# Two cached attentions on one core: Q regrouped by fewer matmuls, one reciprocal for two quads, another table of rankings

## The chip, the cores and the metric

The kernel runs on one core of one Trainium2 chip. The metric is the device time in microseconds (us) of one execution. A time of the kernel is the median of its runs. Engines in the profile: PE is the matmul engine and PEld its weight loads, DVE the vector engine, ACT the scalar engine, POOL the general-purpose engine, SP the engine that issues nearly all loads.

## The reference

Two attention blocks over cached keys and values, each with a query projection and an output projection, side by side in the output. Block A shares each of 4 key/value heads among 8 query heads; block B has 32 key/value heads for its 32 query heads. All inputs and the output are bfloat16.

```python
def _B_ref(x, k_cache, v_cache, wq, wo):        # x: 16 x 32 x 1024
    B, Sq, D = x.shape
    H, Dh = 32, 128                             # k_cache, v_cache: 16 x 32 x 1024 x 128
    q = (x @ wq).reshape(B, Sq, H, Dh).transpose(0, 2, 1, 3)
    scores = jnp.einsum("bhqd,bhkd->bhqk", q, k_cache) * (Dh ** -0.5)
    p = _softmax(scores, axis=-1)
    o = jnp.einsum("bhqk,bhkd->bhqd", p, v_cache)
    return o.transpose(0, 2, 1, 3).reshape(B, Sq, H * Dh) @ wo

# _A_ref: the same with 4 key/value heads, each repeated for 8 query heads
return jnp.concatenate([a, b], axis=-1)         # 16 x 32 x 2048
```

## The kernel before

**Work.** The 512 tokens form 4 groups of 128 (G). Block A has 128 "quads", each the work of one batch entry and 4 query heads (128 rows of scores against 1024 keys). Block B has 128 quads too, taken in pairs: a pair covers two batch entries and four heads. The keys and values of B are read once and used once: 256 K tiles and 256 V tiles of 512 KB each, which are most of the bytes. K tiles of B have 8 slots (`KB_sb`), V tiles 6 (`VB_sb`). In late steps further K and V tiles go into the space of `wq_sb`, `xT_sb`, `QT_sb`, and the last four V tiles into `KB_sb`.

**A quad.** Scores on PE (A: line 995, B: line 1027 on 32x32 tiles of the array, 64 matmuls a pair in four calls), a negated row maximum on DVE (L1038), the exponential on ACT with the row sum as its side output (L1051), transposes of P on PE (A: L1063, B: L1097) with their copies out of PSUM on ACT or DVE (L651), P times V on PE (A: L1083, B: L1116 on 64x64 tiles; the last pair in two halves, L1135), the reciprocal of the sum on DVE (L1165), the scaling by it on ACT or DVE (L1174, L1175), a transposition of the output on PE (A: L1182, B: L1190), and its copy out. B's K tiles are transposed in place by DVE in blocks of 32x32 (L976). After each group the output projection (L823) adds to `acc` (L835, L844); the last adds (L839) are followed by the last stores (L841).

**Sums.** The row maximum, the sum and the reciprocal of every quad lie in one slot of `stat` (8 slots of 4 columns). In B the two quads of a pair share one tile of P (`P2_sb`, one slot, or space in `xT_sb`).

**Q of block B.** For each of the 32 groups of a block of 4 heads, the projected queries (`Qtok`, L754) are transposed by DVE in 32x32 blocks into `QBt` (`qprepB_tr`, L765) and then put into the four row groups that the scores need (`qprepB_sh`, L778): matmuls with a 32x32 corner of the identity as the stationary operand, on 32x32 tiles. They are issued as two operations, `Qshuf` (row groups 0 and 2) and `Qshuf2` (1 and 3), each of 8 matmuls; `Qshuf2` waits on a semaphore for `Qshuf`. Two copies out of PSUM make `QR`.

**Order.** The program is written as a list of 4948 operations. A list scheduler (`list_schedule`) then goes through it on the host and places one operation after the other, with prices written in the code (`DUR`, `PE_MODE`, `MODE_IN`, `MODE_OUT`), slots for the PSUM banks and tiles (`SLOTS`), a model of the load queue and of the fetching of PE's instructions. Among the operations that could start at about the same time it takes the one of highest rank. There are 16 ways of ranking (`RANKS`). Every 77 placed operations (`WINDOW`) a table, `TUNE`, says which of the 16 is used next:

```python
turn = len(order) // WINDOW
turn = TUNE[turn] if turn < len(TUNE) else 0
bl, look, act_first = ranks[turn], RANKS[turn][2], RANKS[turn][4]
```

The result is a fixed order for every engine, with semaphores between engines. SP issues the loads in that order, and waits at a load until the readers of its buffer's last content are done. Such a wait holds every later load.

Of the kernel before, what the change touches and what calls it, by code (L numbers as in the profile page):

```python
# [33 lines left out]
PE_INSTR = {"scoresB": 32, "scoresA": 2, "PT_trA": 8, "PT_trB": 8, "PVA": 16, "PVB": 32, "PVBh": 32, "OT_tr": 2, "OT_trB": 4, "KTA_tr": 16, "Qshuf": 16, "Qshuf2": 16,  # L34
            "qprojA": 4, "qprojB": 4, "oprojA": 4, "oprojB": 4, "xT_tr": 16}
FETCH_BLOCK = 252
FETCH_US = 6.2
# [3 lines left out]
PAIR_COST = 0.01  # L41
FREE_BANKS = 2
WINDOW = 77
RANKS = ((3.5, 122, 0.35, 0.0, 0.3), (3.0, 122, 0.35, 0.0, 0.3), (4.0, 122, 0.35, 0.0, 0.3), (3.5, 122, 0.15, 0.0, 0.3), (2.5, 122, 0.35, 0.0, 0.3), (5.0, 122, 0.35, 0.0, 0.3),
         (3.5, 122, 0.7, 0.0, 0.3), (3.5, 120, 0.35, 0.0, 0.3), (3.0, 124, 0.2, 0.0, 0.3), (3.5, 122, 0.15, 1.5, 0.3), (3.5, 122, 0.15, -1.5, 0.3), (3.5, 122, 0.15, 0.0, 0.0),
         (3.5, 122, 0.15, 0.0, 0.7), (3.5, 122, 0.15, 4.0, 0.3), (3.5, 122, 0.15, -4.0, 0.3), (3.5, 122, 0.25, 0.0, 0.3))
TUNE = (6, 7, 1, 5, 6, 8, 8, 8, 8, 8, 8, 11, 5, 15, 1, 9, 0, 1, 5, 1, 7, 14,
        15, 12, 12, 10, 12, 12, 15, 3, 12, 14, 7, 13, 13, 13, 13, 13, 7, 6, 10, 1, 12, 10,
        3, 12, 0, 11, 9, 12, 7, 13, 12, 11, 12, 3, 4, 10, 14, 9, 9, 10, 4, 0, 0)
HOLD_AHEAD = 1  # L50
STEP_NEAR = 0
TAIL_BASE = 12.0
# [6 lines left out]

DUR = {  # L60
    "scoresB": (0.232, 0.20), "scoresA": (0.216, 0.20), "PT_trA": (0.48, 0.22), "PT_trB": (0.48, 0.22), "PVA": (0.45, 0.22), "PVB": (0.437, 0.22), "PVBh": (0.22, 0.22),
    "OT_tr": (0.056, 0.22), "OT_trB": (0.112, 0.22), "KTA_tr": (0.45, 0.22), "Qshuf": (0.39, 0.20), "Qshuf2": (0.235, 0.20), "qprojA": (0.432, 0.20), "qprojB": (0.432, 0.20),
    "oprojA": (0.432, 0.20), "oprojB": (0.432, 0.20), "xT_tr": (0.45, 0.22),
    "exp": (1.10, 0.12), "PT_ev@act": (0.466, 0.13), "norm@act": (0.25, 0.13), "normB@act": (0.36, 0.13), "OT_ev@act": (0.11, 0.13), "OTB_ev@act": (0.17, 0.13), "KTA_ev@act": (0.466, 0.13),
    "qA_ev@act": (0.47, 0.13), "qB_ev@act": (0.478, 0.13), "QR_ev@act": (0.478, 0.13), "acc0@act": (0.47, 0.13), "acc0@dve": (0.58, 0.12), "xT_ev@act": (0.90, 0.13),
# [46 lines left out]
        self.idx = 0  # L112


SLOTS = {"bank": 8, "P": 2, "P2": 1, "PT": 2, "PT2": 2, "stat": 8, "O": 2, "O2": 3}


def actual(res):
# [9 lines left out]
class Prog:  # L128
# [120 lines left out]
    def list_schedule(self, lat=0.05, look=LOOK):  # L249
# [303 lines left out]
def build(nc, pa, pb, out):  # L553
# [34 lines left out]
    with stack:  # L588
# [49 lines left out]
        pr.add("pool", lambda g: g.memset(rowsel[:], 0.0), writes=["rowsel"], name="c0")  # L638
# [129 lines left out]
        def qprepB_sh(m_, G):  # L768
            gp = (m_ * NG + G) % 2
            vv = [Virt("bank", "pj"), Virt("bank", "pj")]  # L770

            def e_sh(e, aa):
                last = None
                for a in aa:
                    out_ = bank(vv[a // 2])[:, (a % 2) * 2 * Dh:(a % 2 + 1) * 2 * Dh].rearrange("p (hp x) -> p hp x", hp=2)
                    src_ = QBt[32 * a:32 * a + 32, :].rearrange("p (hp e x) -> p e hp x", hp=2, e=2)
                    for rg in range(4):
                        last = e.matmul(out_[32 * rg:32 * rg + 32], ident[32 * a:32 * a + 32, 32 * a:32 * a + 32], src_[:, rg // 2, :, :],  # L778
                                        start=True, stop=True, tile_position=(32 * a, 32 * rg))
                return last  # L780
            for name, aa in (("Qshuf", (0, 2)), ("Qshuf2", (1, 3))):
                pr.add("pe", lambda e, aa=aa: e_sh(e, aa), reads=["QBt", "ident"], writes=vv, claims=[("QR", gp, a) for a in aa], name=name,
                       rtag={"QBt": (m_, G)})
# [225 lines left out]
        def st_scoresB(qs):  # L1009
            n = qs[0].pn  # L1010
            vP, vPT = (("xT", 0, 0), (("xT", 0, 1), ("xT", 0, 2))) if n >= XT_FREE and n % 2 else (Virt("P2"), (Virt("PT2"), Virt("PT2")))
            for q in qs:
                score_buf(q)
                q.vP, q.vPT, q.vO = vP, vPT, Virt("O2")
            q0 = qs[0]
            gp = (q0.m * NG + q0.G) % 2

            def e_s(e, fp):
                last = None
                o0 = (fp // 2) * 64 + fp % 2  # L1020
                for x in range(4):
                    for q in qs:
                        for g2 in range(2):
                            r0 = 32 * (2 * q.e + g2)
                            lhsT = QR[r0:r0 + 32, gp, 2 * q.bp + x // 2, x % 2, o0:o0 + 63:2]
                            rhs = tile_k(4 * q.pn + x)[r0:r0 + 32, :].rearrange("p (s x) -> p s x", s=16)[:, :, o0:o0 + 63:2]
                            last = e.matmul(bank(q.vS[g2])[32 * x:32 * x + 32, :].rearrange("p (s j) -> p s j", s=16), lhsT, rhs,  # L1027
                                            start=(fp == 0), stop=(fp == 3), tile_position=(r0, 32 * x))
# [12 lines left out]
        def st_exp(q):  # L1041
            vS, vP, vst = q.vS, q.vP, q.vst

            def emit(e):
                if q.pi == 0:
                    src = both(vS).rearrange("p u (c k) -> p k u c", c=NCH // 2)
                    dst = P_sb[:, vP.idx, :].rearrange("p (k u c) -> p k u c", u=2, c=NCH // 2)
                else:
                    src = both(vS).rearrange("p g (s j) -> p g j s", s=16)
                    dst = p2_of(vP)[:, q.e * Sk:(q.e + 1) * Sk].rearrange("p (g j s) -> p g j s", g=2, s=16)  # L1050
                return e.activation(dst, src, ACTF.Exp, bias=stat[:, vst.idx, 0:1], scale=1.0, accum_out=stat[:, vst.idx, 1:2])  # L1051
            pr.add("act", emit, writes=vS + [vP, vst], name="exp")

        NPK = NCH // 2

# [67 lines left out]
        def st_last(qs):  # L1123
# [16 lines left out]
            for i in range(2):  # L1140
# [4 lines left out]
                for q in qs:  # L1145
# [1 line left out]
                    if i == 0:  # L1147
                        st_recip(q)

                    def emit(e, i=i, vst=vst, vO=vO, vb=vb):  # L1150
                        dst, src = O2_sb[:, vO.idx, i, :], bank(vb)[:, 0:Dh]
                        if hasattr(e, "activation"):
                            return e.activation(dst, src, ACTF.Copy, scale=stat[:, vst.idx, 2:3])
                        return e.tensor_scalar(dst, src, stat[:, vst.idx, 2:3], None, ALU.mult)
                    eng = ("act", "dve")[q.e]
                    pr.add(eng, emit, reads=[vst], writes=[vb, vO], name="norm@" + eng)
# [5 lines left out]

        def st_recip(q):
            vst = q.vst
            pr.add("dve", lambda e: e.reciprocal(stat[:, vst.idx, 2:3], stat[:, vst.idx, 1:2]), writes=[vst], name="recip")  # L1165

        def st_norm(q):
            vst, vO, vb = q.vst, q.vO, q.vbo

            def emit(e):  # L1170
                dst = O_sb[:, vO.idx, :] if q.pi == 0 else O2_sb[:, vO.idx, :, :].rearrange("p i d -> p (i d)")
                src = bank(vb)[:, 0:Dh if q.pi == 0 else 2 * Dh]
                if hasattr(e, "activation"):
                    return e.activation(dst, src, ACTF.Copy, scale=stat[:, vst.idx, 2:3])  # L1174
                return e.tensor_scalar(dst, src, stat[:, vst.idx, 2:3], None, ALU.mult)  # L1175
            pr.add("any", emit, reads=[vst], writes=[vb, vO], name="norm" if q.pi == 0 else "normB")

        def st_otr(q):
            vO, vb = q.vO, q.vbo
# [223 lines left out]
```

## Time and profile before

| | |
|---|---|
| three runs | 850.86, 853.56, 855.13 us; median 853.56 |
| the profiled execution's own time | 848.26 us |
| its span, first to last instruction | 846.5 us |
| granted clock of PE, mean | 0.998 |
| busy | PE 780.7 us (92%), DVE 727.1 (86%), ACT 623.7 (74%), POOL 6.1 (1%) |
| moved by DMA | 341.68 MB, mean 404 GB/s |
| row maxima L1038 | 256, 1210 ns each |
| K transposes L976 (into `KB_sb`) | 240, 1223 ns each |
| exponentials L1051 (into `P_sb`) | 246, 1123 ns each |
| P times V of B, L1116 | 3584 matmuls with `VB_sb`, 271 ns each |

The span is cut into 40 equal slices in the page; a digit is the busy share of a slice in tenths. Durations of matmuls overlap: PE is a pipeline, and a matmul's row shows how long one took from its start to its modelled end, while the next may have begun. The chain of waits follows the work that ended last back to the start, step by step, to what released it. A group's row reads: line, engine, operation, output and inputs, shapes, how many | busy time, mean ns of one | idle time of the engine just before them, and what ended it. A timeline's row reads: start in us, length in us, engine, line, operation, how many were merged, and in brackets the idle time before.

### The profile page before, as it was taken

What the parts mean: (1) busy time and instruction counts of PE and PEld (TensorE: products, weight loads), DVE (VectorE), ACT (ScalarE), POOL (GpSimd) and SP (SyncE); (2) the same over time, 40 slices, a digit from 0 to 9 for tenths busy, and PEclk for the clock granted to TensorE, in tenths of its full rate; (3) what the DMA queues carried; (4) which work ended last, traced back from release to release, by engine and by line L of the source; (5) the groups of instructions that cost most, each with busy time, mean ns of one, the idle gap of its engine ahead of it and who ended that gap; (6) DMA issues with size and microseconds to landing.
All of it is one profiled execution on the core that took longest, in us unless ns stands there. A gap on an engine that the chain in (4) does not pass through costs nothing.

```text
span 846.5 us, 29749 instructions
## 1 busy us (share of the span) xinstructions
PE 780.7 (92%) x13056; PEld 520.6 (62%) x13056; DVE 727.1 (86%) x1018; ACT 623.7 (74%) x1363; POOL 6.1 (1%) x20
## 2 busy tenths in 40 slices
PE   6989999999998999898999998999899998889878
PEld 3456665666665666565666665566666665566655
DVE  1499978979989898986999888998899879998995
ACT  3488787778777677777778787577867868686874
POOL 1000000000000000000000000000000000000000
PEclk9999999999999999999999999999999999999999
DMA  9999999999999999999999999999999999999995
GB/s 333 415 412 415 411 412 413 406 398 392 415 415 412 414 405 415 411 403 412 415 404 409 405 395 416 415 413 406 410 405 413 413 414 415 415 412 413 415 418 212
DMA packets 112208, 341.68 MB, mean 404 GB/s; under 512 B 12048, under 2 KB 12304, under 8 KB 112080
## 3 DMA queue, kind: packets, MB, share of 16 engines
q1 hardware_dynamic: 111520, 337.95, 100.1%
q8 instruction: 103, 1.69, 0.7%
q0 software_dynamic: 560, 1.84, 0.5%
q14 instruction: 25, 0.20, 0.1%
HBM read 337.64 MB, written 2.10 MB: 401 GB/s over the span
## 4 chain that ended last, share of the span: by engine, by line
PE 51%; DVE 22%; ACT 13%; DMA 11%; issue 2%; SPq 1%; DVEq 0%; ACTq 0%
DVE stat L1038 10%; PE psum L1116 9%; DVE KB_sb L976 8%; ACT P_sb L1051 7%; PE psum L823 7%; DMA KB_sb<-in_B_k_cache_dram 7%; PE psum L1027 5%; PE psum L735 5%; PE psum L1063 5%; PE psum L754 5%; PE psum L995 4%; PE psum L1083 4%; PE psum L1097 4%; DMA wq_sb<-in_B_k_cache_dram 2%; ACT PT_sb L651 2%
## 5 line engine op out<-in xcount | busy, mean ns | idle before, releaser
L1038 DVE TENSOR_REDUCE stat<-psum 128x1 f32<-128x1024 f32 x256 | 303.6, 1210 | 48.9 <-PE psum L995 29.2
L1051 ACT ACTIVATE P_sb<-psum,stat 128x1024 bf16<-128x1024 f32 x246 | 276.0, 1123 | 64.0 <-DVE stat L1038 60.3
L976 DVE STREAM_TRANSPOSE KB_sb<-KB_sb 128x1024 f32<-128x1024 f32 x240 | 286.8, 1223 | 8.5 <-DMA KB_sb<-in_B_k_cache_dram 8.0
L651 ACT COPY PT_sb<-psum 128x512 f32<-128x512 f32 x226 | 131.4, 604 | 34.9 <-PE psum L1063 22.0
L1116 PE MATMUL psum<-VB_sb,PT_sb 64*64 64x256 bf16 x3584 | 115.4, 271 | 7.3 <-ACT P_sb L1051 5.1
L1116 PEld LDWEIGHTS psum<-VB_sb,PT_sb 64*64 64x64 bf16 x3584 | 96.9, 107 | 25.6 <-issue 23.6
L1174 ACT ACTIVATE O_sb<-psum,stat 128x128 bf16<-128x128 f32 (+1 forms) x205 | 80.8, 417 | 42.1 <-PE psum L1083 21.7
L1063 PE MATMUL psum<-id,P_sb 128*128 128x128 f32 x512 | 89.0, 298 | 6.5 <-ACT P_sb L1051 4.5
L1063 PEld LDWEIGHTS psum<-id,P_sb 128*128 128x128 f32 x512 | 74.1, 208 | 24.7 <-ACT P_sb L1051 14.4
L995 PE MATMUL psum<-KTA_sb,QT_sb 128*128 128x512 bf16 x256 | 83.8, 381 | 3.5 <-ACT P_sb L1051 2.0
L1083 PE MATMUL psum<-VA_sb,PT_sb 128*128 128x128 bf16 x1024 | 78.3, 220 | 7.5 <-ACT P_sb L1051 2.8
L1083 PEld LDWEIGHTS psum<-VA_sb,PT_sb 128*128 128x128 bf16 x1024 | 62.5, 98 | 31.5 <-issue 11.1
L1027 PE MATMUL psum<-KB_sb,QR 32*32 32x512 bf16 x3840 | 73.3, 394 | 8.0 <-ACT P_sb L1051 3.6
L1097 PE MATMUL psum<-id,P_sb 128*128 128x128 f32 x472 | 75.7, 285 | 4.1 <-ACT P_sb L1051 3.5
L754 PE MATMUL psum<-wq_sb,xT_sb 128*128 128x512 bf16 x256 | 71.5, 389 | 3.4 <-DMA wq_sb<-in_B_wq_dram 1.6
L1097 PEld LDWEIGHTS psum<-id,P_sb 128*128 128x128 f32 x472 | 63.5, 193 | 17.3 <-ACT P_sb L1051 7.5
L823 PE MATMUL psum<-woB_sb,OTB_sb 128*128 128x512 bf16 x256 | 66.9, 380 | 2.3 <-ACT P_sb L1051 1.6
L1027 PEld LDWEIGHTS psum<-KB_sb,QR 32*32 32x32 bf16 x3840 | 43.6, 89 | 35.3 <-ACT P_sb L1051 8.0
L823 PE MATMUL psum<-woA_sb,OTA_sb 128*128 128x512 bf16 x256 | 62.8, 380 | 0.4 <-ACT OTA_sb L651 0.3
L735 PE MATMUL psum<-xT_sb,wq_sb 128*128 128x512 bf16 x192 | 54.2, 380 | 1.9 <-issue 1.2
L1051 ACT ACTIVATION_READ_ACCUMULATOR P_sb<-psum,stat 128x1 f32 x246 | 50.4, 205 | 0.0
L835 DVE TENSOR_TENSOR acc<-acc,psum 128x512 f32<-128x512 f32 x64 | 41.3, 675 | 8.9 <-PE psum L823 8.8
(74 smaller groups left out, 719.6 us busy)
## 6 DMA issues: line engine op xcount, KB each, us to landing
KB_sb<-in_B_k_cache_dram SPq DMA_DIRECT2D x240, 512.0 KB, 9.7
VB_sb<-in_B_v_cache_dram SPq DMA_DIRECT2D x234, 512.0 KB, 8.6
KA_sb<-in_A_k_cache_dram SPq DMA_DIRECT2D x64, 256.0 KB, 8.5
VA_sb<-in_A_v_cache_dram SPq DMA_DIRECT2D x64, 256.0 KB, 8.5
wq_sb<-in_B_wq_dram SPq DMA_DIRECT2D x16, 512.0 KB, 8.4
woB_sb<-in_B_wo_dram SPq DMA_DIRECT2D x32, 256.0 KB, 9.7
woA_sb<-in_A_wo_dram SPq DMA_DIRECT2D x32, 256.0 KB, 7.9
wq_sb<-in_B_k_cache_dram SPq DMA_DIRECT2D x16, 512.0 KB, 12.0
```

The lines of the kernel that those rows point to most:

```text
L651: return e.copy(dst, src) if hasattr(e, "activation") else e.tensor_copy(dst, src)
L754: last = e.matmul(bank(v)[:, 0:CW], xT_sb[:, 1, j, G * P:(G + 1) * P], wq_sb[:, j, mh * CW:(mh + 1) * CW], start=(j == 0), stop=(j == DJ - 1))
L823: last = e.matmul(bank(v)[:, 0:OUTW], OT[:, gp, hh, :], wo_[:, hh, oh * OUTW:(oh + 1) * OUTW], start=(hh == 0), stop=(hh == nh - 1))
L976: pr.add("dve", lambda e: e.transpose(tile_k(x).bitcast(F32), tile_k(x).bitcast(F32)), writes=[home_k(x)], name="KBt_tr", rtag={home_k(x): ...
L995: pr.add("pe", lambda e, u=u: e.matmul(bank(vS[u]), qt[:, q.b, q.hh0:q.hh0 + 4, :].rearrange("p a q -> p (a q)"), KTA_sb[:, sl, u * 512:(u ...
L1027: last = e.matmul(bank(q.vS[g2])[32 * x:32 * x + 32, :].rearrange("p (s j) -> p s j", s=16), lhsT, rhs, start=(fp == 0), stop=(fp == 3), t ...
L1038: pr.add("dve", lambda e: e.tensor_reduce(stat[:, vst.idx, 0:1], both(vS), AXIS.XY, ALU.max, negate=True), writes=vS + [vst], name="max")
L1051: return e.activation(dst, src, ACTF.Exp, bias=stat[:, vst.idx, 0:1], scale=1.0, accum_out=stat[:, vst.idx, 1:2])
L1063: last = e.transpose(bank(vb)[:, m * P:(m + 1) * P], p32[:, m:Sk // 2:NPK], id32[:])
L1083: last = e.matmul(bank(vb)[:, 0:Dh], ptc_of(vPT, c, 0, P), VA_sb[:, kvs, c, :], start=(c == 0), stop=(c == NCH - 1))
L1097: last = e.transpose(bank(vb)[:, m * P:(m + 1) * P], p32[:, 4 * h + m:Sk:8], id32[:])
L1116: last = e.matmul(bank(q.vbo)[n0:n0 + 64, 0:2 * Dh].rearrange("p (i d) -> p i d", i=2), pt2_chunk(vPT, c, e0, n0), v2[e0:e0 + 64, :, c, :] ...
```

## The change

Three things change.

1. `qprepB_sh`: each matmul fills two row groups at once. A new constant `idd` holds two 32x32 identities side by side for each of the four row blocks; it is made by 8 copies on POOL ahead of `rowsel`. A preparation has 8 matmuls on 32x64 tiles where it had 16 on 32x32 tiles.
2. The sums of a pair of B go into one slot of a new tile `rs` (4 slots of 4 columns). The reciprocals of both quads are one instruction on two columns, issued for the first quad; the scalings read from `rs`.
3. `TUNE` is another table, with 85 entries in place of 65. From the 4620th placed operation on (`FINE`), the ranking may change every 11 operations (`FINE_WINDOW`) rather than every 77. The scheduler's counts and prices of `Qshuf` and `Qshuf2` are changed too.

```diff
-... "Qshuf": 16, "Qshuf2": 16,
+... "Qshuf": 8, "Qshuf2": 8,
...
+FINE = 4620
+FINE_WINDOW = 11
...
-TUNE = (6, 7, 1, 5, 6, 8, 8, 8, 8, 8, 8, 11, 5, 15, 1, 9, 0, 1, 5, 1, 7, 14,
...
+TUNE = (6, 11, 1, 10, 2, 2, 3, 2, 10, 14, 2, 15, 4, 4, 4, 4, 4, 3, 8, 14, 2, 2,
...
-    ... "Qshuf": (0.39, 0.20), "Qshuf2": (0.235, 0.20), ...
+    ... "Qshuf": (0.30, 0.20), "Qshuf2": (0.17, 0.20), ...
...
-SLOTS = {"bank": 8, "P": 2, "P2": 1, "PT": 2, "PT2": 2, "stat": 8, "O": 2, "O2": 3}
+SLOTS = {"rs": 4, "bank": 8, "P": 2, "P2": 1, "PT": 2, "PT2": 2, "stat": 8, "O": 2, "O2": 3}
...
-            turn = len(order) // WINDOW
+            turn = len(order) // WINDOW if len(order) < FINE else FINE // WINDOW + (len(order) - FINE) // FINE_WINDOW
...
+        rs = sb("rs", [P, SLOTS["rs"], 4], F32)
+        idd = sb("idd", [P, 64], BF)
...
+        for r_ in range(4):
+            pr.add("pool", lambda g, r_=r_: g.tensor_copy(idd[...][:, 0, :], ident[32 * r_:32 * r_ + 32, 32 * r_:32 * r_ + 32]), ...)
+            pr.add("pool", lambda g, r_=r_: g.tensor_copy(idd[...][:, 1, :], ident[32 * r_:32 * r_ + 32, 32 * r_:32 * r_ + 32]), ...)
...
-                    for rg in range(4):
-                        last = e.matmul(out_[32 * rg:32 * rg + 32], ident[32 * a:32 * a + 32, 32 * a:32 * a + 32], src_[:, rg // 2, :, :],
-                                        start=True, stop=True, tile_position=(32 * a, 32 * rg))
+                    for hf in range(2):
+                        last = e.matmul(out_[64 * hf:64 * hf + 64], idd[32 * a:32 * a + 32, :], src_[:, hf, :, :],
+                                        start=True, stop=True, tile_position=(32 * a, 64 * hf))
...
-                return e.activation(dst, src, ACTF.Exp, bias=stat[:, vst.idx, 0:1], scale=1.0, accum_out=stat[:, vst.idx, 1:2])
-            pr.add("act", emit, writes=vS + [vP, vst], name="exp")
+                return e.activation(dst, src, ACTF.Exp, bias=stat[:, vst.idx, 0:1], scale=1.0, accum_out=stat[:, vst.idx, 1:2] if q.pi == 0 else rs[:, q.vrs.idx, q.e:q.e + 1])
+            pr.add("act", emit, reads=[] if q.pi == 0 else [vst], writes=vS + [vP] + ([vst] if q.pi == 0 else [q.vrs]), name="exp")
...
+            if q.pi == 0:
+                pr.add("dve", lambda e: e.reciprocal(stat[:, vst.idx, 2:3], stat[:, vst.idx, 1:2]), writes=[vst], name="recip")
+            elif q.e == 0:
+                pr.add("dve", lambda e: e.reciprocal(rs[:, q.vrs.idx, 2:4], rs[:, q.vrs.idx, 0:2]), writes=[q.vrs], name="recip")
+
+        def inv(q):
+            return stat[:, q.vst.idx, 2:3] if q.pi == 0 else rs[:, q.vrs.idx, 2 + q.e:3 + q.e]
```

More of the change, by code (lines that the diff above doesn't have):

```diff
@@ L33 @@
 MODE_OUT = {0: 0.0, 2: 0.18, 3: 0.1}
-PE_INSTR = {"scoresB": 32, "scoresA": 2, "PT_trA": 8, "PT_trB": 8, "PVA": 16, "PVB": 32, "PVBh": 32, "OT_tr": 2, "OT_trB": 4, "KTA_tr": 16, "Qshuf": 16, "Qshuf2": 16,
+PE_INSTR = {"scoresB": 32, "scoresA": 2, "PT_trA": 8, "PT_trB": 8, "PVA": 16, "PVB": 32, "PVBh": 32, "OT_tr": 2, "OT_trB": 4, "KTA_tr": 16, "Qshuf": 8, "Qshuf2": 8,
             "qprojA": 4, "qprojB": 4, "oprojA": 4, "oprojB": 4, "xT_tr": 16}
@@ L46 @@
          (3.5, 122, 0.15, 0.0, 0.7), (3.5, 122, 0.15, 4.0, 0.3), (3.5, 122, 0.15, -4.0, 0.3), (3.5, 122, 0.25, 0.0, 0.3))
-TUNE = (6, 7, 1, 5, 6, 8, 8, 8, 8, 8, 8, 11, 5, 15, 1, 9, 0, 1, 5, 1, 7, 14,
-        15, 12, 12, 10, 12, 12, 15, 3, 12, 14, 7, 13, 13, 13, 13, 13, 7, 6, 10, 1, 12, 10,
-        3, 12, 0, 11, 9, 12, 7, 13, 12, 11, 12, 3, 4, 10, 14, 9, 9, 10, 4, 0, 0)
+TUNE = (6, 11, 1, 10, 2, 2, 3, 2, 10, 14, 2, 15, 4, 4, 4, 4, 4, 3, 8, 14, 2, 2,
[3 rows of a table added]
 HOLD_AHEAD = 1
@@ L61 @@
     "scoresB": (0.232, 0.20), "scoresA": (0.216, 0.20), "PT_trA": (0.48, 0.22), "PT_trB": (0.48, 0.22), "PVA": (0.45, 0.22), "PVB": (0.437, 0.22), "PVBh": (0.22, 0.22),
-    "OT_tr": (0.056, 0.22), "OT_trB": (0.112, 0.22), "KTA_tr": (0.45, 0.22), "Qshuf": (0.39, 0.20), "Qshuf2": (0.235, 0.20), "qprojA": (0.432, 0.20), "qprojB": (0.432, 0.20),
+    "OT_tr": (0.056, 0.22), "OT_trB": (0.112, 0.22), "KTA_tr": (0.45, 0.22), "Qshuf": (0.30, 0.20), "Qshuf2": (0.17, 0.20), "qprojA": (0.432, 0.20), "qprojB": (0.432, 0.20),
     "oprojA": (0.432, 0.20), "oprojB": (0.432, 0.20), "xT_tr": (0.45, 0.22),
@@ L636, in build @@
                    writes=[key], name="c1")
-        pr.add("pool", lambda g: g.memset(rowsel[:], 0.0), writes=["rowsel"], name="c0")
+        for r_ in range(4):
+            pr.add("pool", lambda g, r_=r_: g.tensor_copy(idd[32 * r_:32 * r_ + 32, :].rearrange("p (h x) -> p h x", h=2)[:, 0, :], ident[32 * r_:32 * r_ + 32, 32 * r_:32 * r_ + 32]),
+                   reads=["ident"], writes=["idd"], name="c1")
+            pr.add("pool", lambda g, r_=r_: g.tensor_copy(idd[32 * r_:32 * r_ + 32, :].rearrange("p (h x) -> p h x", h=2)[:, 1, :], ident[32 * r_:32 * r_ + 32, 32 * r_:32 * r_ + 32]),
+                   reads=["ident"], writes=["idd"], name="c1")
+        pr.add("pool", lambda g: g.memset(rowsel[:], 0.0), reads=["idd"], writes=["rowsel"], name="c0")
         for r_ in range(4):
@@ L776, in e_sh @@
                     src_ = QBt[32 * a:32 * a + 32, :].rearrange("p (hp e x) -> p e hp x", hp=2, e=2)
-                    for rg in range(4):
-                        last = e.matmul(out_[32 * rg:32 * rg + 32], ident[32 * a:32 * a + 32, 32 * a:32 * a + 32], src_[:, rg // 2, :, :],
-                                        start=True, stop=True, tile_position=(32 * a, 32 * rg))
+                    for hf in range(2):
+                        last = e.matmul(out_[64 * hf:64 * hf + 64], idd[32 * a:32 * a + 32, :], src_[:, hf, :, :],
+                                        start=True, stop=True, tile_position=(32 * a, 64 * hf))
                 return last
             for name, aa in (("Qshuf", (0, 2)), ("Qshuf2", (1, 3))):
-                pr.add("pe", lambda e, aa=aa: e_sh(e, aa), reads=["QBt", "ident"], writes=vv, claims=[("QR", gp, a) for a in aa], name=name,
+                pr.add("pe", lambda e, aa=aa: e_sh(e, aa), reads=["QBt", "idd"], writes=vv, claims=[("QR", gp, a) for a in aa], name=name,
                        rtag={"QBt": (m_, G)})
@@ L1011, in st_scoresB @@
             vP, vPT = (("xT", 0, 0), (("xT", 0, 1), ("xT", 0, 2))) if n >= XT_FREE and n % 2 else (Virt("P2"), (Virt("PT2"), Virt("PT2")))
+            vrs = Virt("rs")
             for q in qs:
                 score_buf(q)
-                q.vP, q.vPT, q.vO = vP, vPT, Virt("O2")
+                q.vP, q.vPT, q.vO, q.vrs = vP, vPT, Virt("O2"), vrs
             q0 = qs[0]
@@ L1148, in st_last, with emit @@
                         st_recip(q)
-                    def emit(e, i=i, vst=vst, vO=vO, vb=vb):
+                    def emit(e, i=i, q=q, vO=vO, vb=vb):
                         dst, src = O2_sb[:, vO.idx, i, :], bank(vb)[:, 0:Dh]
                         if hasattr(e, "activation"):
-                            return e.activation(dst, src, ACTF.Copy, scale=stat[:, vst.idx, 2:3])
-                        return e.tensor_scalar(dst, src, stat[:, vst.idx, 2:3], None, ALU.mult)
+                            return e.activation(dst, src, ACTF.Copy, scale=inv(q))
+                        return e.tensor_scalar(dst, src, inv(q), None, ALU.mult)
                     eng = ("act", "dve")[q.e]
-                    pr.add(eng, emit, reads=[vst], writes=[vb, vO], name="norm@" + eng)
+                    pr.add(eng, emit, reads=[q.vrs], writes=[vb, vO], name="norm@" + eng)
                     pr.add("pe", lambda e, i=i, vO=vO, vb=vb: e.matmul(bank(vb)[:, 256:384], O2_sb[:, vO.idx, i, :], rowsel[:, i, :], start=True, stop=True),
@@ L1164, in st_recip @@
             vst = q.vst
-            pr.add("dve", lambda e: e.reciprocal(stat[:, vst.idx, 2:3], stat[:, vst.idx, 1:2]), writes=[vst], name="recip")
+            if q.pi == 0:
[4 more added lines that the diff above has]
+            return stat[:, q.vst.idx, 2:3] if q.pi == 0 else rs[:, q.vrs.idx, 2 + q.e:3 + q.e]
         def st_norm(q):
@@ L1173, in emit @@
                 if hasattr(e, "activation"):
-                    return e.activation(dst, src, ACTF.Copy, scale=stat[:, vst.idx, 2:3])
-                return e.tensor_scalar(dst, src, stat[:, vst.idx, 2:3], None, ALU.mult)
-            pr.add("any", emit, reads=[vst], writes=[vb, vO], name="norm" if q.pi == 0 else "normB")
+                    return e.activation(dst, src, ACTF.Copy, scale=inv(q))
+                return e.tensor_scalar(dst, src, inv(q), None, ALU.mult)
+            pr.add("any", emit, reads=[vst if q.pi == 0 else q.vrs], writes=[vb, vO], name="norm" if q.pi == 0 else "normB")
         def st_otr(q):
```

3 rows, old and new, of the table TUNE are left out of this document.

## The prediction

> **What bounds the kernel now.** I read the page first, then the busy time by windows (forty slices, then 5 us at the end and 2 us around one dip), then the waits of the queue that issues the loads, then the groups by form and the timelines of the edited lines.
>
> ```profile
> span 846.5 us, 29749 instructions
> DMA  9999999999999999999999999999999999999995
> GB/s 333 415 412 415 411 412 413 406 398 392 415 415 412 414 405 415 411 403 412 415 404 409 405 395 416 415 413 406 410 405 413 413 414 415 415 412 413 415 418 212
> DMA packets 112208, 341.68 MB, mean 404 GB/s; under 512 B 12048, under 2 KB 12304, under 8 KB 112080
> PE 51%; DVE 22%; ACT 13%; DMA 11%; issue 2%; SPq 1%; DVEq 0%; ACTq 0%
> ```
>
> The DMA engines are full in every slice but the last. 341.68 MB at 415 GB/s, the rate of the undisturbed slices, take 823.3 us. The span is 23.2 us more, and the windows of 2 us say where: some 4 us at the start before the loads run, some 10 us after 830 us, and a net 8 to 9 us in between, in dips under 405 GB/s. The chain of waits (last line) hardly names DMA and gives PE half: loads and compute are abreast, and the compute's order decides when buffers come free. But no faster compute moves bytes faster: what can be won is the dips, some 8 us, and a little of the end.
>
> One dip, by windows (the last two columns are DMA share and GB/s):
>
> ```profile
> 188.00:190.00 2.00, 2.00 (x90) 1.68 (x64) 1.84 (x3) 0.36 (x1) 0.00 (x0) 1.00 0.98 335
> ...
> 194.00:196.00 2.00, 2.00 (x14) 1.25 (x12) 2.00 (x5) 2.00 (x7) 0.00 (x0) 1.00 0.89 322
> ```
>
> And the issuing queue's waits, first the longest from 182 to 198 us, then the largest of the whole span (total, times, longest):
>
> ```profile
> SPq L910 <- PE psum L1027: 5.1, 1, 5.1
> ...
> SPq L955 <- PE psum L1116: 107.7, 37, 6.7
> ```
>
> One 5.1 us wait of SP for a score matmul (it frees a K buffer) precedes the dip. From 188 to 196 us the four rates 335, 346, 373, 322 lose (80+69+42+93)/415 x 2 = 1.4 us. Most waits of SP, 107.7 us in 37 for PV alone, lose nothing, since loads still queue behind.
>
> The end, in windows of 5 us (PE first, DMA share and GB/s last), and SP's last issue of loads:
>
> ```profile
> 825.00:830.00 5.00, 5.00 (x92) 2.35 (x94) 4.79 (x6) 2.88 (x5) 0.00 (x0) 1.00 1.02 415
> 830.00:835.00 5.00, 5.00 (x123) 4.56 (x119) 2.48 (x9) 4.13 (x9) 0.54 (x1) 1.00 0.80 323
> 835.00:840.00 5.00, 4.75 (x171) 3.33 (x161) 1.32 (x4) 2.00 (x8) 0.00 (x0) 1.00 0.20 79
> ```
>
> ```profile
> 818.99 3.63 SPq L955 DMA_DIRECT2D KB_sb<-in_B_v_cache_dram  x4
> ```
>
> Loads stay full to 830 us, thin out, and the last four V tiles (issued by 822.6, 15.3 us median to landing) arrive near 837.5. Then the last PV half, projection, adds and store take 9 us that must follow the last byte. From 830 to 837.5 us about 1.1 + 2.0 = 3.1 us of transfer time are lost ((415-323)/415 x 5, and the same for 79 GB/s over 2.5 us): the issues of the last loads came a little late.
>
> **The Q regrouping.** Each of 32 preparations has two sets of 8 matmuls; they become two sets of 4, which is 256 matmuls and as many weight loads fewer (of 13056 each). The groups of the two edited operations, and timeline rows of PE:
>
> ```profile
> L778 PE MATMUL psum<-QBt,ident 32*32 32x256 bf16 x512 | 20.0, 277 | 3.2 <-issue 0.4 <-ACT P_sb L1051 0.3
> ...
> L1165 DVE RECIPROCAL stat<-stat 128x1 f32<-128x1 f32 x256 | 30.5, 146 | 11.7 <-ACT P_sb L1051 10.1
> ```
>
> ```profile
> 38.20 0.69 PE L778 MATMUL psum<-QBt,ident 32*32 32x256 bf16 x16
> 38.82 0.62 PE L969 MATMUL psum<-ident,KA_sb 128*128 128x128 bf16 x8
> ...
> 697.32 1.21 PE L1027 MATMUL psum<-KB_sb,QR 32*32 32x512 bf16 x64
> 698.27 0.73 PE L778 MATMUL psum<-QBt,ident 32*32 32x256 bf16 x16
> ...
> 819.66 0.30 PE L778 MATMUL psum<-QBt,ident 32*32 32x256 bf16 x8
> ```
>
> A set of 8 spans 0.30 us where one matmul alone is 0.28: the starts are 3 ns apart, and the set already runs side by side. Both sets span 0.69, so the second starts 0.39 after the first: it waits for the first on a semaphore, and that wait stays. The next matmul starts 0.62 after the block began. Taking out 4 starts of 3 ns in each of 64 sets saves 64 x 0.012 = 0.8 us of PE. The other bound is the pace at which PE is fed in a long block: 64 score matmuls in 1.21 us, one of 0.39 among them, make (1.21 - 0.39)/63 = 13 ns each; 256 fewer are 3.3 us. I take 0.8 us, the row of the operation itself.
> The Trainium skill, "TensorE: Matmul & The Clock Gate" (section "Wait — 56ns, not 53.3ns?"), says that matmuls never start closer than about 25 ns. By it the cut would be an estimated 256 x 25 ns = 6.4 us of PE, and the sum 2.9 us lower (half of 5.6 more); the 3 ns starts above speak against it here.
>
> Tiles of 32x64 are another shape than the scores' 32x32. At 10 places of the PE timeline a set directly follows scores (as at 698.27): it starts 0.26 us before their end (697.32 + 1.21 - 698.27), against 0.06 at 38.20, behind a full-array matmul that ends at 38.26. Losing that overlap costs 10 x 0.20 = 2.0 us; if it stays, nothing. I take the loss.
> "TensorEngine Tiling (Array Packing)", section "Tiling Modes", of the Trainium skill says the same, that changing the tiling mode drains the array; no run here shows it between these two shapes.
>
> PE's net is thus +1.2 us; half of it on the path, as PE holds 51% of the chain: +0.6.
>
> **One reciprocal for two quads.** 64 of 256 DVE instructions go. A lone one is 146 ns, but five in a row take 0.40 us, so 80 ns each: 64 x 0.08 = 5.1 us of DVE; reading two columns instead of one is nothing beside 128x1 at the same fixed cost. DVE holds 22% of the chain: -1.1 us. The merged one waits for both exponentials; behind it on DVE stand maxima and K transposes. That is no new wait: the second quad's own reciprocal had it (10.1 us in 11 waits), and both PV operands already needed both exponentials, which share one P tile. The sum slots (4) outnumber the P2 tile (1) and the tiles of the late pairs, so none is waited for.
>
> **Setup.** Eight more POOL copies of some 0.2 us (four ran in 1.0 us) end by 5.5 us; the first regrouping is at 38.20, and `rowsel`, now behind them, is read only after the first PV. Nothing; it would cost under 2 us if anything early read them.
>
> **Instruction supply.** 2% of PE's instructions go; the pieces named "issue" add up to 14.8 us of the chain, so -0.3.
>
> **The table.** All operations may change place, and from the 4,620th on (the last 272 of 4,892, roughly from 793 us) the ranking changes every 11. It adds no work. Its reach is bounded from both sides by the ledger: -8 us (no dips) -3 us (the end) at best, though a shorter body would itself leave a thin end; and as many more late releases at worst, +8 us. By the same windows PE stood idle 4.3 us from 805 to 825 us while DVE was busy throughout, just where the last V loads wait for buffers; that is where finer choices act. I take half of the 3.1 us there, -1.5, and zero for the body, whose sign no row gives.
>
> Sum: 0.6 - 1.1 - 0.3 - 1.5 = -2.3 us, against the profiled execution's 848.26 us (span 846.5). The three runs have a median of 853.56, 5.3 above that execution, so I put the difference on the median: 853.56 - 2.3 = 851.3, given as 851.
>
> **The rivals.** (1) The dips go: a new order issues K loads before the ring thins. For it: a late release stands before the dip shown, and there DVE was not full, so order alone could mend it. Against it: PE is 92% busy and nothing large is removed. Price: -8 us, 845.5.
> (2) A new wait of SP: one score group or one PV placed a few us later than now, repeated in the steady pattern. The dip at 188 cost 1.4 us for one 5.1 us wait; four more such are +5.6 us, 859. It decides once SP waits so long that its queue (9.7 us from issue to landing) runs dry, four or more times more often than now. For it: waits up to 7.0 us exist already, the order is planned from fixed prices, and a plan that knows no drain may put the regrouping behind scores more often. Against it: the bytes are the same, and most waits cost nothing.
> (3) The starts, not the semaphore, are the price of the regrouping. For it: the 13 ns feed. Against it: the 3 ns starts. Price: half of 3.3 - 0.8 more on the path, 850.
> The rule of the Trainium skill named above ("TensorE: Matmul & The Clock Gate") has the same mechanism at twice the size and would give 848.4.
> (4) The change does not do what it says: the sets last as long, the order lands where it was, the loads set the time: 853.5.
>
> **How the numbers follow.** 0.5%, 4.3 us, is about what a measurement of this kernel can tell from no change. The forecast case has 0.42, with its own range 846.5 to 855, of which 0.11 lies below 849.3 and 0.31 within the bound. Dips gone 0.22, all faster. A new wait 0.28, all slower. Dear starts 0.06, of which 0.02 faster and 0.04 within. Nothing done 0.02, within. So faster 0.35, same 0.37, slower 0.28. The range reaches from 843.5 (all dips and part of the end) to 860 (four to five new dips); a tenth lies beyond each end.
>
> **What would show it.** Right: L778 with 256 matmuls of about 0.28 us, the second set still 0.39 us after the first; 192 reciprocals; DMA at 1.03 in nearly every slice, the last loads landing 1 to 3 us earlier with 9 us behind them. Wrong: a block of L778 well under 0.5 us; more slices under 405 GB/s; SP waits of 6 us and over in number; or a stretch behind the last landing that differs from 9 us.

## The result and the profile after

The kernel after takes 872.58 us (median of 4 runs, 871.84 to 873.01) against 853.24 us before (4 runs): the ratio is 1.0236, 95% interval 1.021 to 1.0263. By the medians it is 19.3 us slower, and outside the predicted range, which ended at 860.

The profiled execution took 872.2 us, with a span of 870.3. These are the lines of its page that answer to those of before: the span, the busy share of the DMA engines and the rate in 40 slices, the bytes, and the chain of waits by engine.

```profile
span 870.3 us, 29173 instructions
...
DMA  9999999999999999999999999999999999999994
GB/s 331 403 401 405 405 399 407 398 395 403 404 392 401 405 376 358 405 401 400 406 405 401 400 398 392 404 372 404 400 404 404 402 404 405 405 406 403 407 407 180
DMA packets 112206, 341.65 MB, mean 393 GB/s; under 512 B 12048, under 2 KB 12304, under 8 KB 112080
...
PE 41%; DMA 31%; DVE 13%; ACT 9%; issue 3%; SPq 3%; DVEq 0%; ACTq 0%
```

The second row is as full as before, and the bytes are the same. The third row is the finding: a full slice moves at 405 GB/s, where it moved at 415. The best slices of after, 406 and 407, lie below nearly all undisturbed slices of before. At that rate 341.65 MB take 843.6 us, 20.3 more than the 823.3 of before. The span is 23.8 us longer; the other 3.5 us show in slices such as 376, 358 and 372, which have no counterpart of that size before. In the chain, DMA went from 11% to 31%: the compute now waits for loads.

The groups by form show the same from the compute's side, after first and then before (line, engine, operation, shapes, how many | busy, mean ns | idle before, released by):

```profile
L987 DVE STREAM_TRANSPOSE KB_sb<-KB_sb 128x1024 f32<-128x1024 f32 x240 | 288.9, 1226 | 29.0 <-DMA KB_sb<-in_B_k_cache_dram 27.8
L1050 DVE TENSOR_REDUCE stat<-psum 128x1 f32<-128x1024 f32 x256 | 303.2, 1210 | 39.8 <-PE psum L1039 22.4 <-PE psum L1006 16.4
L1178 DVE RECIPROCAL stat<-stat 128x1 f32<-128x1 f32 x128 | 18.3, 146 | 7.4 <-ACT P_sb L1063 6.8
L1180 DVE RECIPROCAL rs<-rs 128x2 f32<-128x2 f32 x64 | 9.4, 146 | 2.0 <-ACT P_sb L1063 1.7
L789 PE MATMUL psum<-QBt,idd 32*64 32x256 bf16 x256 | 19.3, 292 | 2.1
```

```profile
L976 DVE STREAM_TRANSPOSE KB_sb<-KB_sb 128x1024 f32<-128x1024 f32 x240 | 286.8, 1223 | 8.5 <-DMA KB_sb<-in_B_k_cache_dram 8.0
```

DVE's waits for K tiles went from 8.0 to 27.8 us, while the operations themselves kept their lengths (a K transpose 1226 ns after 1223, a maximum 1210 both times). So these operations did not become slower; the loads did. The counts of the edits are as announced: 256 matmuls at L789, 128 + 64 reciprocals, and a reciprocal of two columns takes the 146 ns of one.

Why would the same loads move more slowly? Two theories.

**Address theory.** The two new tiles, `rs` (64 B a partition) and `idd` (128 B), stand among the old ones, and tiles lie one behind the other. Before, 896 B of small tiles came first, and the allocator's base stands 128 B past a multiple of 1024; so `xT_sb` and all large tiles behind it began on multiples of 1024 B. After, `xT_sb`, `wq_sb` and `QT_sb` lie 64 B past one, and `QR`, `wo`, `acc`, K and V lie 192 B past one. **Order theory.** The new table gives another order, and another mix of loads in flight moves more slowly.

### The profile page after: what moved, and what is told of

Its sections match the earlier page's. It is cut to its first block, busy times and chain, and to the rows that moved or that the text cites. A ratio compares the mean times of both kernels' runs of the same rounds, so it can differ in the third digit from the quotient of the medians.

```text
span 870.3 us, 29173 instructions
## 1 busy us (share of the span) xinstructions
PE 787.6 (90%) x12800; PEld 519.9 (60%) x12800; DVE 729.3 (84%) x951; ACT 625.8 (72%) x1366; POOL 7.8 (1%) x28
## 2 busy tenths in 40 slices
DMA packets 112206, 341.65 MB, mean 393 GB/s; under 512 B 12048, under 2 KB 12304, under 8 KB 112080
## 4 chain that ended last, share of the span: by engine, by line
PE 41%; DMA 31%; DVE 13%; ACT 9%; issue 3%; SPq 3%; DVEq 0%; ACTq 0%
DMA KB_sb<-in_B_k_cache_dram 14%; DMA VB_sb<-in_B_v_cache_dram 11%; PE psum L1128 9%; DVE stat L1050 6%; ACT P_sb L1063 6%; PE psum L834 5%; DVE KB_sb L987 5%; PE psum L1039 5%; PE psum L746 4%; PE psum L1075 3%; DMA VA_sb<-in_A_v_cache_dram 3%; PE psum L1109 3%; PE psum L1095 3%; PE psum L1006 3%; PE psum L765 2%
## 5 line engine op out<-in xcount | busy, mean ns | idle before, releaser
L1050 DVE TENSOR_REDUCE stat<-psum 128x1 f32<-128x1024 f32 x256 | 303.2, 1210 | 39.8 <-PE psum L1039 22.4
L987 DVE STREAM_TRANSPOSE KB_sb<-KB_sb 128x1024 f32<-128x1024 f32 x240 | 288.9, 1226 | 29.0 <-DMA KB_sb<-in_B_k_cache_dram 27.8
L662 ACT COPY PT_sb<-psum 128x512 f32<-128x512 f32 x216 | 125.2, 600 | 27.8 <-PE psum L1075 17.5
L1075 PEld LDWEIGHTS psum<-id,P_sb 128*128 128x128 f32 x512 | 73.4, 208 | 24.5 <-ACT P_sb L1063 10.4
L1006 PE MATMUL psum<-KTA_sb,QT_sb 128*128 128x512 bf16 x256 | 80.7, 382 | 6.0 <-ACT xT_sb L1063 2.3
L1109 PEld LDWEIGHTS psum<-id,P_sb 128*128 128x128 f32 x472 | 62.1, 194 | 17.4 <-ACT P_sb L1063 8.0
L1192 ACT ACTIVATE O_sb<-psum,stat 128x128 bf16<-128x128 f32 x119 | 44.6, 376 | 27.0 <-PE psum L1095 23.8
L1192 ACT ACTIVATE O_sb<-psum,rs 128x256 bf16<-128x256 f32 x89 | 39.4, 475 | 26.6 <-PE psum L1128 23.8
L746 PE MATMUL psum<-xT_sb,wq_sb 128*128 128x512 bf16 x192 | 51.9, 383 | 0.8 <-ACT QR L662 0.5
```

Source lines behind the costliest of these rows:

```text
L662: return e.copy(dst, src) if hasattr(e, "activation") else e.tensor_copy(dst, src)
L987: pr.add("dve", lambda e: e.transpose(tile_k(x).bitcast(F32), tile_k(x).bitcast(F32)), writes=[home_k(x)], name="KBt_tr", rtag={home_k(x): ...
L1006: pr.add("pe", lambda e, u=u: e.matmul(bank(vS[u]), qt[:, q.b, q.hh0:q.hh0 + 4, :].rearrange("p a q -> p (a q)"), KTA_sb[:, sl, u * 512:(u ...
L1050: pr.add("dve", lambda e: e.tensor_reduce(stat[:, vst.idx, 0:1], both(vS), AXIS.XY, ALU.max, negate=True), writes=vS + [vst], name="max")
L1075: last = e.transpose(bank(vb)[:, m * P:(m + 1) * P], p32[:, m:Sk // 2:NPK], id32[:])
L1109: last = e.transpose(bank(vb)[:, m * P:(m + 1) * P], p32[:, 4 * h + m:Sk:8], id32[:])
```

## Experiments: where the targets lie

The ratio of an experiment is to runs of the kernel before that were made beside it; their medians lie between 851.20 and 852.25 us.

**The new tiles at the end.** Every older tile lies where it was; the order is that of after.

```diff
-        rs = sb("rs", [P, SLOTS["rs"], 4], F32)
-        idd = sb("idd", [P, 64], BF)
...
         O_sb = sb("O_sb", [P, SLOTS["O"], Dh], BF)
+        rs = sb("rs", [P, SLOTS["rs"], 4], F32)
+        idd = sb("idd", [P, 64], BF)
```

> The kernel after, with the two new tiles (rs of 64 B and idd of 128 B a partition) taken after all others, so that every older tile lies where it lay before the change. Address theory (the loads are slower because their targets in SBUF moved by 64 and 192 B): the full slices return from 405 to 415 GB/s, a 4 KB packet from a median near 161 ns to 159 ns, and the time falls from 872.6 to about 850 us (872.6 - 20.3 of transfer = 852, plus or minus 3). Order theory (the new table's order of loads and of compute makes the loads slower): nothing moves, 872 us and 405 GB/s.

Measured: 854.74 us, ratio to before 1.0035 (1.0016 to 1.0053). Its slices:

```profile
span 853.6 us, 29051 instructions
...
GB/s 327 416 412 416 414 412 416 393 390 403 415 389 412 415 409 358 410 413 411 414 410 413 413 412 354 416 378 413 412 415 417 409 411 415 416 416 415 415 417 199
```

Full slices are back at 415. About 17 of the 19 us go with two lines that were moved. What is left, some 3 us (0.35%), shows in single slices: 358, 354, 378.

**The old kernel, shifted.** Nothing but two unused tiles.

```diff
         stat = sb("stat", [P, SLOTS["stat"], 4], F32)
+        pad0 = sb("pad0", [P, 16], F32)
...
         QBt = sb("QBt", [P, CW], BF)
+        pad1 = sb("pad1", [P, 64], BF)
```

> The kernel before, with two unused tiles of 64 B and 128 B a partition put where rs and idd stand after the change. Order and all instructions are those of before. Address theory: full slices at 405 GB/s, time 853 + 20 = about 873 us (868 to 876). Order theory: 853 us at 415 GB/s.

Measured: 871.4 us, ratio 1.0238 (1.0215 to 1.026), the ratio of the change itself.

```profile
span 868.6 us, 29624 instructions
...
GB/s 333 403 401 404 405 396 375 401 397 393 405 405 400 402 402 404 399 398 400 405 392 400 392 395 405 405 397 397 401 406 401 399 404 406 406 387 401 408 408 200
```

With order and instructions of before, 405 GB/s. The order theory falls for the 19 us: the address is sufficient (here) and necessary (the run above). In the trace's packet records, packets of 4 KB that took 160 ns or less are 99% before, 40% after and 41% here.

**How large an offset, and which.** Each is the kernel before with one unused tile behind `stat`, of 128, 32 or 256 B a partition:

```diff
+        pad0 = sb("pad0", [P, 32], F32)    # 128 B; 8 and 64 columns in the other two
```

> The kernel before, with one unused tile of 128 B a partition ahead of the large tiles: all targets of loads lie 128 B past a multiple of 256 B and of 1024 B. Address theory with the offset as price: between 853 and 873 us, slices between 405 and 415 GB/s. If only whole multiples of 64 B and less matter (128 being as good as 0): 853 us. Order theory: 853 us. By the Trainium skill, page DMA: Bandwidth & Descriptors, section How a descriptor splits into AXI transactions, the wasted part is the offset itself, an estimated 128/4096 = 3% of a 4 KB packet and twice that of a 2 KB packet, which would be an estimate of some 30 us.

> The kernel before, with one unused tile of 32 B a partition ahead of the large tiles: all targets lie 32 B past a multiple of 256 B. If any offset costs the same (one more piece to each packet): as b_shift, about 873 us. If the cost grows with the offset: a small part of it, 853 to 859 us. Order theory: 853 us.

> The kernel before, with one unused tile of 256 B a partition ahead of the large tiles; it lay on multiples of 1024 B and now lies 256 B past them. If multiples of 256 B are what a packet needs (128 cost 18.6 us, 32 cost 21): 852 us, 415 GB/s. If a packet needs more (512 or 1024): about 870 us.

| offset past a multiple of 1024 B | time | ratio to before (95%) | full slices, GB/s |
|---|---|---|---|
| 32 B | 873.3 us | 1.0261 (1.0234 to 1.0288) | 403 to 406 |
| 128 B | 870.76 us | 1.0225 (1.0202 to 1.0248) | 404 to 407 |
| 256 B | 852.56 us | 1.0001 (0.9979 to 1.0022) | 414 to 417 |

A start 256 B past a multiple of 1024 B is as good as one on it, and each of the two smaller offsets costs about the same, 2.2 to 2.6%. The Trainium skill, "DMA: Bandwidth & Descriptors", section "How a descriptor splits into AXI transactions", says that transactions start on 256 B boundaries, and that a transfer that begins between two is read from the boundary below, at the cost of the bytes ahead. The page speaks of reading, and what moved here is the end that is written. The boundary agrees with these runs. The size does not: that cost would grow with the offset, and 32 B cost no less than 128, for which 18.6 us were measured and not the estimated 30. A price that is the same for every offset, the first case of the expectation for 32 B, is what fits; its cause, such as one more piece to each packet, is in no trace.

**Only tiles that no load writes.**

```diff
         VA_sb = sb("VA_sb", [P, 2, NCH, Dh], BF)
+        pad0 = sb("pad0", [P, 16], F32)
```

> The kernel before, with one unused tile of 64 B a partition behind the last tile that a load writes (VA_sb): only tiles that engines alone read and write (KTA, P, PT, O) move by 64 B. If the targets of loads are the cause: 852 us. If the engines' own operands at such places are slower, or disturb the loads: up to 871 us.

Measured: 852.11 us, ratio 1.0002 (0.9984 to 1.0019). With the engines' own tiles (`KTA`, `P`, `PT`, `O`) 64 B past a multiple of 256 B, no loss can be measured.

**The weights' tiles alone, and the K and V tiles alone.** In the first run the tiles of weights, `x` and `acc` lie 64 B past a multiple of 256 B, and K and V on one:

```diff
         stat = sb("stat", [P, SLOTS["stat"], 4], F32)
+        pad0 = sb("pad0", [P, 16], F32)
...
+        pad1 = sb("pad1", [P, 48], F32)
         KB_sb = sb("KB_sb", [P, NKB, 16 * Dh], BF)
```

In the second, K and V lie 192 B past one, and everything ahead of them in its old place:

```diff
+        pad1 = sb("pad1", [P, 48], F32)
         KB_sb = sb("KB_sb", [P, NKB, 16 * Dh], BF)
```

> The kernel before, with 64 B a partition ahead of the large tiles and 192 B ahead of KB_sb: xT, wq, QT, wo and acc lie 64 B past a multiple of 256 B, the K and V tiles again on one. About 54 of 338 MB go to moved tiles (84 MB in b_shift's other part would be 284). Address theory, with the price in proportion to the bytes moved: 0.16 x 19 = 3 us, 854 to 857 us. If one moved tile slows all loads: 865 us or more.

> The kernel before, with one unused tile of 192 B a partition ahead of KB_sb: the K and V tiles lie 192 B past a multiple of 256 B, as after the change; xT, wq, QT, wo and acc stay on multiples of 1024 B. 284 of 338 MB go to moved tiles. Address theory in proportion to the bytes: 0.84 x 19 = 16 us, 868 us. If the weights' tiles carry none of it (b_shiftw came out within 0.1%): the whole 19 us, 871 us, with full slices at 405 GB/s, except where late K and V tiles go into the space of wq, xT and QT, which stays in place: the last slices keep 415 for those.

Measured: 851.58 us, ratio 1.0011 (0.9988 to 1.0034), for the weights' side; 864.19 us, 1.0149 (1.0117 to 1.0181), for K and V. The slices of the second run:

```profile
GB/s 341 407 409 404 403 406 394 407 396 407 404 392 407 403 395 405 406 406 407 402 395 407 406 400 406 405 397 402 407 406 403 401 409 410 410 394 406 412 414 193
```

K and V tiles, 84% of the bytes, carry most of it. The last slices rise to 412 and 414, where late K and V tiles go into the unmoved space of `wq`, `xT` and `QT`, as expected. But both expected sizes were missed: the parts, about 0.1% and 1.5%, do not add up to the 2.4% of the whole. Both 868 and 871 us were outside. In the packet records of the second run 59% of the 4 KB packets took 160 ns or less, against 41% with everything moved. Moved weight tiles seem to cost only when K and V are moved too; why is open.

## Experiments: the edits and the order

These look for the 3 us that were left, and test the terms of the prediction's sum. In all of them the new tiles, where there are any, lie at the end.

**The regrouping alone, order kept.**

```diff
-                    for rg in range(4):
-                        last = e.matmul(out_[32 * rg:32 * rg + 32], ident[...], src_[:, rg // 2, :, :], ...)
+                    for hf in range(2):
+                        last = e.matmul(out_[64 * hf:64 * hf + 64], idd[32 * a:32 * a + 32, :], src_[:, hf, :, :], ...)
```

> The kernel before with the regrouping on 32x64 tiles alone, every engine's order kept (the copies that make idd are made in the operations that fill rowsel, and idd lies at the end). If the semaphore wait sets a preparation and the change of tile shape costs 0.2 us at 10 places: 852.2 + 0.6 = 852.8 us. If each matmul start costs 13 to 25 ns: 850.5 to 849 us. If nothing of it is on the path: 852.2 us.

Measured: 850.73 us, ratio 0.9998 (0.998 to 1.0016). Nothing of it is on the path that can be measured; an effect of 0.6 us would be too small to see, a gain of 2 us or more lies outside the interval. The timeline of PE at the place that the prediction showed at 697 us:

```profile
698.30 1.22 PE L1032 MATMUL psum<-KB_sb,QR 32*32 32x512 bf16 x64
699.46 0.68 PE L783 MATMUL psum<-QBt,idd 32*64 32x256 bf16 x8
700.07 0.40 PE L1195 MATMUL psum<-rowsel,O_sb 128*128 128x128 bf16 x4
```

Two readings. The block still spans 0.68 us and its successor starts 0.61 later, where the block at 38.20, also behind another tile shape, had 0.69 and 0.62: halving the matmuls saved 0.01. And it starts 0.06 us before the scores end (698.30 + 1.22 - 699.46), where on equal tiles it started 0.26 before: the overlap across the change of tile shape is lost, 0.20 us, as taken. At all ten places where a set follows scores the start lies 0.06 to 0.08 us before their end in this run, and 0.10 to 0.27 in the profile of before; together they lose 1.6 us of overlap, where the prediction took 2.0. That also answers what was open about the rule on draining cited from the Trainium skill ("TensorEngine Tiling (Array Packing)", "Tiling Modes"): between 32x32 and 32x64 tiles these rows agree with it.

**Both edits, old table.** The kernel after, with the table of before:

```diff
-FINE = 4620
+FINE = 10 ** 9
-TUNE = (6, 11, 1, 10, 2, 2, 3, 2, 10, 14, ...
+TUNE = (6, 7, 1, 5, 6, 8, 8, 8, 8, 8, ...
```

> The kernel after with the new tiles at the end, and with the old table of rankings, one way for each 77 operations; both edits and their prices stay. If the new table makes the 3 us that a_tail lies above before: 849 to 852 us. If the edits make them (a drained array between the two tile shapes): 854 to 857 us. By the prediction's sum without its -1.5 for the table: 852.2 - 0.8 = 851.4 us.

Measured: 865.66 us, ratio 1.0163 (1.0136 to 1.0189). All three expectations missed: with the old table the edited kernel is 11 us slower than with the new one. Full slices move at 415; the loss lies in dips:

```profile
GB/s 324 415 412 415 408 411 417 415 340 389 416 413 407 411 408 410 392 407 398 415 392 373 413 413 414 404 402 368 413 416 412 416 411 412 417 416 391 388 409 123
```

Either the edits cost 14 us, or the order does. So:

**Both edits, every engine's order kept as before.** The order is made from the old list; then the second (or first) reciprocal of each pair is left out of it.

```diff
+            skip.add(l[r2][1] if late_exp < r1 else l[r1][1])    # per pair of quads
         for k in seq:
+            if k in skip:
+                continue
```

> The kernel before with both edits (regrouping on 32x64 tiles, one reciprocal for two quads) and with the order of every engine kept as it was before, the second reciprocal of each pair left out of it; the new tiles lie at the end, so no target of a load moves. If the 14 us of e_edits come from the new order that the old table gives to a shorter list, and not from the edits: 849 to 852 us, with dips as before (some 9 us under 405 GB/s). If the merged reciprocal itself holds DVE or the scalings: 855 us or more.

Measured: 851.69 us, ratio 1.0008 (0.9988 to 1.0028).

```profile
span 848.4 us, 29181 instructions
...
GB/s 324 415 413 413 415 406 396 399 390 393 415 416 412 414 404 415 408 407 412 417 411 411 408 395 417 416 415 412 400 403 411 413 415 414 414 411 412 416 418 208
```

The edits as such cost nothing and win nothing that can be measured. The 14 us came with the order that the old table gives to the changed list, which has 64 reciprocals fewer, 8 copies more and other prices for `Qshuf`. Every later entry of the table then meets other operations; which of the differences matters was not separated.

**The new table alone, on the old list.**

```diff
+FINE = 4620
+FINE_WINDOW = 11
-TUNE = (6, 7, 1, 5, 6, 8, 8, 8, 8, 8, ...
+TUNE = (6, 11, 1, 10, 2, 2, 3, 2, 10, 14, ...
```

> The kernel before with the new table of rankings and its finer windows alone; list of operations, prices and tiles are those of before. If a table only suits the list it was made for: 856 to 868 us, with more dips under 405 GB/s than before. If the new table is better or worse by itself: like a_tail, 853 to 856 us.

Measured: 883.18 us, ratio 1.038 (1.0344 to 1.0416), worse than expected. The rows are DMA share and rate by slices, and then, from the waits of SP's queue, the one with the longest single wait:

```profile
DMA  9996999999999999999999999699999999999993
GB/s 338 414 411 219 415 413 417 414 415 412 413 361 413 370 399 357 413 407 413 415 415 402 388 374 400 232 390 413 413 413 410 404 414 415 416 416 414 416 417 128
```

```profile
SPq L913 <- PE psum L1030: 59.1, 26, 12.4
```

Two slices at 219 and 232 GB/s lose about 10 us each ((415-219)/415 x 22). One wait of SP for a score matmul, in the second of them, lasted 12.4 us, longer than the 8.8 us that its loads take from issue to landing: the queue ran dry, and from 558 to 562 us only 3 GB/s moved.

A smaller dip of this kind stands in the run with the tiles at the end. Windows of 4 us around the slice of 358 (the last three figures are PE's granted clock, DMA share and GB/s), and SP's longest waits from 305 to 340 us:

```profile
308.00:312.00 4.00, 1.66 (x17) 0.83 (x19) 2.12 (x2) 1.44 (x2) 0.00 (x0) 0.88 1.04 417
312.00:316.00 4.00, 3.98 (x27) 2.20 (x26) 2.79 (x7) 2.46 (x8) 0.00 (x0) 0.69 1.03 421
316.00:320.00 4.00, 3.95 (x30) 2.60 (x31) 3.67 (x6) 2.96 (x6) 0.00 (x0) 1.00 1.01 385
320.00:324.00 4.00, 4.00 (x20) 1.75 (x18) 4.00 (x6) 2.87 (x6) 0.00 (x0) 1.00 1.03 412
324.00:328.00 4.00, 3.54 (x89) 2.40 (x87) 2.29 (x5) 2.42 (x7) 0.00 (x0) 1.00 0.71 249
328.00:332.00 4.00, 3.50 (x85) 3.15 (x83) 4.00 (x5) 4.00 (x10) 0.00 (x0) 1.00 0.93 342
332.00:336.00 4.00, 3.76 (x85) 2.10 (x84) 4.00 (x7) 1.84 (x6) 0.00 (x0) 1.00 0.96 354
```

```profile
SPq L902 <- PE psum L1006: 8.2, 1, 8.2
SPq L921 <- PE psum L1039: 5.9, 1, 5.9
```

SP stood 8.2 us at a load of `KA_sb`, held by a score matmul of A, and then 5.9 us at a K tile of B; the thin stretch from 324 to 336 us cost (166 + 73 + 61)/415 x 4 = 2.9 us. Ahead of the first wait PE itself stood still: inside a group of B's scores it was idle for 2.01 us, up to 309.43, with nothing that the profile shows to wait for ("issue"), and its granted clock then fell to 0.88 and 0.69 (the first two rows). In the profile of after PE stands at the same group, and waits of SP of 8.3 and 5.9 us follow:

```profile
315.63 0.40 PE L1039 MATMUL psum<-KB_sb,QR 32*32 32x512 bf16 x4 [2.37 <-issue]
```

So the late scores are not only a matter of where the new order puts them. Nor does it take the new order: in the profile of the 256 B run, with the order of before, PE stood 1.89 us inside a score group at 117 us, its clock fell to 0.67, a load of V then waited 9.4 us, and two windows moved at 250 and 332 GB/s, a loss of 2.4 us. That run as a whole equals the kernel before (1.0001); the profiled execution, 855.80 us, was the slowest of its ten. That this dip makes the 3 us of the change that are not address is likely from its size, and not shown.

No version here beats the kernel before: the regrouping alone (0.9998) and both edits in the old order (1.0008) equal it.

## Why the prediction was wrong

**The step that failed** is the first one: "341.68 MB at 415 GB/s, the rate of the undisturbed slices, take 823.3 us" was carried over to the kernel after, together with the setup's price of nothing. "No faster compute moves bytes faster" is true, and it was read as if nothing in the change could move them more slowly. The sum took 415 GB/s as a constant and looked for changes only in dips and ends. The 415 were a property of where the tiles lie: after the change full slices moved at 405, at which the bytes take 843.6 us, 20.3 more. "Setup" priced what the new tiles take to fill (8 copies on POOL), and not what they push aside. Measured: about 17 to 19 us by the runs that undo it or do it alone (ratio 1.0236 against 1.0035; 871.4 us against 852.16). No term stood for it in the sum, none of the rivals named it, and the range ended at 860 because the largest loss considered was four or five more dips.

**Slower, but for another reason.** The rival of a new wait of SP (859 us, chance 0.28) had the right sign, and by luck. Waits of its kind are there once the tiles are in place, 8.2 and 5.9 us with a dip of 2.9 us, but behind a stall of PE that the rival did not name, and whether they make the 3 us that are left is not shown. They are not what made the change slower by 19 us.

**The regrouping** was right in mechanism: a set of 8 ran side by side already, the semaphore sets the block (0.62 us before, 0.61 after), and the change of tile shape takes up to 0.20 us of overlap. The two sizes were both somewhat large, 2.0 us for the overlap (1.6 by the ten places) and 0.8 us for the starts (0.01 a block, an estimated 0.3 for 32), so that PE's net of +1.2 us comes out at an estimated +1.3. The net of +0.6 us is below what the runs can tell (0.9998, 0.998 to 1.0016). The starts as the price, the rival with the 13 ns feed, would have gained about 1.7 us and is just at the edge of that interval; the 25 ns of the Trainium skill's rule ("TensorE: Matmul & The Clock Gate", "Wait — 56ns, not 53.3ns?"), worth some 3 us, lie beyond it.

**The reciprocals** were sized at -1.1 us by DVE's share of the chain. Both edits in the old order came to 1.0008 (0.9988 to 1.0028), an interval of some -1.0 to +2.4 us. The sum of -0.8 us for all that the edits do lies just inside it, and is too small to be told from nothing.

**The table** was bounded by +8 and -11 us, and taken at -1.5. The best comparisons say otherwise: old table on the new list +14 us, new table on the old list +32, new table on its own list +3. The prediction's count of today's dips bounds the gain, not the loss: one wait longer than a load takes to land costs up to 10 us by itself. The last loads did not land earlier either: the transfer thins out from 850 us on in after and the last V tile lands near 862.8, with 7.5 us behind it where 9 were forecast.

## What to carry to other kernels

When a change adds a tile, work out where every tile behind it now lies, above all the targets of loads: here two tiles of 64 and 128 B cost 17 to 19 us, where all the instructions of the change cost nothing that could be measured, and moving two declarations gave some 17 us back. When the rate of full DMA slices differs between two profiles of the same bytes, look at addresses before looking at order. A table that steers a scheduler by position belongs to one list of operations: test an edit in a kept order, or the table's misfit is taken for the edit's cost.

## What was not expected of the hardware

- Loads into tiles that begin on a multiple of 256 B ran at 415 GB/s in full slices; 32 B or 128 B past one, or 64 B for weights with 192 B for K and V, at about 405: 2.2 to 2.6% of the kernel's time. The share of busy DMA time, 1.03, looks the same in both.
- Moving only the K and V tiles cost 1.5%, only the weights' tiles 0.1%, both 2.4%. This is not explained; a run with the same offset for all parts, one part at a time, was not made.
- A matmul set on 32x64 tiles did not overlap the end of one on 32x32 tiles (0.06 to 0.08 us at ten places, against 0.10 to 0.27 on equal tiles).
